# Fewer, larger last transfers, the last V product ahead of the MLP product, and set-up work moved off VectorE, in a decode kernel of attention and MLP

## The chip, the cores and the metric

One NeuronCore of a Trainium2 chip runs the whole program, once. The metric is the device time of one execution in microseconds (us). Before the change three runs gave 722.03 to 722.25 us, median 722.1 us.

## The reference, cut to what matters

Two rows of `x` (B = 2) pass through a decode step of multi-head attention (32 heads of 128, 4096 cached keys and values for each head) and through a dense MLP with a tanh-approximated GELU; a sigmoid gate mixes the two.

```python
q = (x @ wq) split into 32 heads                       # x [2,1,576], wq [576,4096]
p = softmax(einsum("bhqd,bhkd->bhqk", q, k_cache) * 128**-0.5)   # k_cache [2,32,4096,128]
a = einsum("bhqk,bhkd->bhqd", p, v_cache) flattened @ wo         # wo [4096,576]
b = gelu(x @ w1 + b1) @ w2 + b2                        # w1 [576,4608], w2 [4608,576]
g = sigmoid((x * gate_w).sum(-1))
out = g * a + (1 - g) * b
```

All of it is fp32. The K and V caches are 134 MB each, the weights together 40 MB.

## The kernel before, in words

**One ring of three slots.** SBUF holds one tile `ring` with three slots of 64 KB per partition. The weights wq and w1 fill its front first. After that every transfer of the list `seq` takes the next slot: K and V of unit 0, of unit 1, up to unit 15 (a unit is four heads of one batch row, 8.4 MB of K and as much of V), and last three slots named in `LAST`, which hold w2 and wo. All these transfers are issued from SyncE (SP) in that order. A transfer may be issued when the slot that it writes is free: `load_next` is called behind the work that reads a slot for the last time. The first `LAST` slot takes V of unit 14's place, the second K of unit 15's, the third V of unit 15's.

**A unit.** VectorE multiplies K with q in place (`mul`, L510), GpSimd halves a part of the product (L514), VectorE adds up the rest (`red`, L515 and L516) and takes the maximum (L520); TensorE turns it (`mt`, L525), ScalarE takes the exponentials into the tile `p` (`softmax`, L535), and TensorE multiplies them with V in 32 matmuls of 512 columns (`av`, L546; a matmul in fp32 shows as two passes, so 64). `keep` (L558) and `combine` (L564) fold the result into the tile `oall`. The product with V of unit k is made beside the K work of unit k + 1.

**The set-up.** SP issues wq and w1 in five transfers, ScalarE (ACT) issues the first part of b1, the two rows of x and gate_w. x is transposed on TensorE (`xps`, L270) once gate_w is there, then come the projections to q (`qps`, L303) and to the MLP's hidden row (`hps`, L303), with the GELU in `hg`. Constants such as `idsc`, the zeroed `p` and `rs` and `ones` are made on VectorE.

**The separate half row of w2.** The last of each partition's 36 rows of w2 is loaded only in its first half as part of the block; the other halves (128 half rows of 288) are loaded apart, into `XP` partitions with `XS` half rows in each (`wx`, from `XC` transfers over `XE` partitions). The hidden values that belong to them have to be laid out the same way, in `hx`: before, VectorE makes the two patterns `mod` and `div` and the masked product `hm`, and one matmul gathers it (L416).

**The tail.** After the 15th unit's `max_n` and `softmax` TensorE's program is written out by hand: `mlp_out(lo, hi)` multiplies hg with rows lo to hi of w2 (four passes a row), `mlp_x` does the separate half rows (two passes each), `norm_sum`, `norm_t` and `o_turn` normalise and turn the attention output between pieces of `mlp_out`, `wo_out(0, 23)` multiplies it with the first 23 rows of wo, and `last_out` does rows 23 to 31 into `res` and writes the output. All of `mlp_out`, `mlp_x` and `wo_out` are line L367 with the tile `acc`.

Of the kernel before, what the change touches and what calls it, by code (L numbers as in the profile page):

```python
# [8 lines left out]
F32 = mybir.dt.float32  # L9
AF = mybir.ActivationFunctionType  # L10
ALU = mybir.AluOpType
AX = mybir.AxisListType
P = 128
# [6 lines left out]
def kernel(  # L20
# [14 lines left out]
    nc = tc.nc  # L35
    B, H, SK, DH = k_cache.shape
# [21 lines left out]
    NF = F // P  # L58
# [4 lines left out]
    SCALE = float(DH) ** -0.5  # L63
# [1 line left out]

    LAST = (
        (("w2", 0, 14), ("w2", 14, 28)),
        (("w2", 28, 36), ("wx", 0, 1), ("wo", 0, 8), ("wo", 8, 16)),
        (("wo", 16, 23), ("wo", 23, 27), ("wo", 27, 30), ("wo", 30, 31), ("wo", 31, 32)),
    )  # L70
    FOLD = 23
    SLOT = R * DH
# [17 lines left out]
    ps_sm = ctx.enter_context(tc.tile_pool(name="ps_sm", bufs=3, space=bass.MemoryType.PSUM))  # L90
# [18 lines left out]
    def load_w(w, rows, c):  # L109
        if c < len(rows):  # L110
            n = rows[c] * w.shape[1]
            lo = sum(rows[:c]) * P
            src = w[lo:lo + rows[c] * P].rearrange("(p r) n -> p (r n)", r=rows[c])
        else:
            n = w.shape[1] // 2
            src = w[NX * P:].rearrange("q (e n) -> (q e) n", e=2)
        t = ring[:, used["w"]:used["w"] + n]
        used["w"] += n
        nc.sync.dma_start(t, src)
        return t  # L120
# [5 lines left out]
    def load_heads(src, i):  # L126

        t = slot(SLOT)
        h = i // B * E
        nc.sync.dma_start(t, src[i % B, h:h + E].rearrange("h (p r) d -> (h p) (r d)", p=PE_))  # L130
        return t.rearrange("p (r d) -> p r d", d=DH)

    srcs = {"w2": w2.rearrange("(p r) n -> p (r n)", r=NF), "wo": wo.rearrange("(p r) n -> p (r n)", r=32)}

    XE, XC = 4, 4
    XP = XE * XC
    XS = P // XP
    srcx2 = w2.rearrange("(e c s r) n -> c r e s n", e=XE, c=XC, s=XS)[:, NF - 1, :, :, DS:]
# [4 lines left out]
    def load_last(m):  # L143
        n = sum(length(*q) for q in LAST[m])

        used["e"], used["z"] = len(held) % SLOTS * SLOT + n, (len(held) % SLOTS + 1) * SLOT
        t = slot(n)
        o = 0
        for w, a, z in LAST[m]:
            if w == "wx":  # L150
                xt = t[:XP, o:o + XS * DS]
                rows[w] = xt.rearrange("p (s n) -> p s n", s=XS)
                o += XS * DS
                for c in range(XC):
                    nc.sync.dma_start(xt[c::XC].rearrange("e (s n) -> e s n", s=XS), srcx2[c])
                continue
            if (w, z) == ("w2", NF):
                nc.sync.dma_start(t[:, o:o + length(w, a, z)], srcs[w][:, a * D:z * D - DS])
                for r in range(a, z):
                    rows[w, r] = t[:, o + (r - a) * D:o + min((r - a + 1) * D, length(w, a, z))]  # L160
                o += length(w, a, z)
                continue

            ends = (a * D, a * D + DS, a * D + DS + DO, z * D) if (w, z) == ("wo", 32) else (a * D, z * D)
            for u, v in zip(ends, ends[1:]):
                nc.sync.dma_start(t[:, o:o + v - u], srcs[w][:, u:v])
                o += v - u
            for r in range(a, z):
                rows[w, r] = t[:, o - (z - r) * D:o - (z - r - 1) * D]

    def temp(n, parts=P):
        t = ring[:parts, used["t"]:used["t"] + n]
        used["t"] += n
        assert used["t"] <= SLOTS * SLOT
        return t

    def late(n, parts=P):
        t = ring[:parts, used["e"]:used["e"] + n]
        used["e"] += n
        assert not seq and used["e"] <= used["z"]  # L180
        return t

    def load():
        if not seq:
            return
        kind, i = seq.pop()
        if kind == "wq":
            wqt[i] = load_w(wq, ROWS[kind], i)
        elif kind == "w1":
            w1t[i] = load_w(w1, ROWS[kind], i)  # L190
        elif kind == "k":
            kt[i] = load_heads(k_cache, i)
        elif kind == "v":
            vt[i] = load_heads(v_cache, i)
        else:
            load_last(i)
        if kind in ("k", "v", "last"):
            held.append((kind, i))
# [7 lines left out]
    xg = temp(D, B + 1)  # L206
# [8 lines left out]
    def load_b1(b):  # L215
        nc.scalar.dma_start(b1r.rearrange("(g q) n -> g q n", g=NG)[:, b], b1.rearrange("(g n) -> g n", g=NG))


    load_b1(0)
    for b in range(B):  # L220
        nc.scalar.dma_start(xg[b:b + 1], x[b])
    nc.scalar.dma_start(xg[B:B + 1], gate_w[None, :])
    load()
    load()
# [2 lines left out]
    ident = cp.tile([P, P], F32, name="ident")  # L227
    make_identity(nc, ident)
    ones = cp.tile([P, 1], F32, name="ones")
    nc.vector.memset(ones, 1.0)  # L230
    idsc = cp.tile([P, P], F32, name="idsc")
    nc.vector.tensor_scalar_mul(idsc, ident, SCALE)


    NPB = 1
# [3 lines left out]
    pt = []  # L239
    for j in range(NPB):  # L240
        t = cp.tile([P, NT * EB + 32 - EB], F32, name=f"p{j}")
        nc.vector.memset(t, 0.0)
        pt.append(t)
    rs = cp.tile([P, NO], F32, name="rs")
    nc.vector.memset(rs, 0.0)


    sel = ident.rearrange("p (j c) -> p j c", j=4)[:, :, :EB].rearrange("p j (e r) -> p j e r", e=E)
# [114 lines left out]
    def acc_mm(lhsT, rhs, k, start=False, stop=False, lo=0):  # L363
        m = lhsT.shape[-1]
        for s in range(lo, lo + rhs.shape[-1] // DS):
            o = 64 * (k % 2) + 32 * s
            nc.tensor.matmul(  # L367
                acc[o:o + m], lhsT, rhs[:, (s - lo) * DS:(s - lo + 1) * DS], start=start, stop=stop, skip_group_check=True
            )
# [19 lines left out]
    for m, ps in enumerate(hps):  # L389
# [7 lines left out]
    hg = cp.tile([P, NF, B], F32, name="hg")  # L397
    t = temp(NF * B).rearrange("p (r b) -> p r b", b=B)
# [5 lines left out]
    nc.vector.tensor_mul(t, t, hb)  # L404
    nc.vector.tensor_mul(hg, t, g1.unsqueeze(1).to_broadcast([P, NF, B]))

    mod = temp(XS)
    nc.vector.tensor_reduce(mod, ident.rearrange("p (q s) -> p s q", s=XS), AX.X, ALU.add)
    div = temp(XP)
    nc.vector.tensor_reduce(div, ident.rearrange("p (q s) -> p q s", s=XS), AX.X, ALU.add)  # L410
    hm = temp(XS * B).rearrange("p (s b) -> p s b", b=B)
    nc.vector.tensor_mul(
        hm, hg[:, NF - 1:].to_broadcast([P, XS, B]), mod.unsqueeze(2).to_broadcast([P, XS, B])
    )
    hxps = ps_sm.tile([XP, XS * B], F32, tag="sm", name="hxps")
    nc.tensor.matmul(hxps, div, hm.rearrange("p s b -> p (s b)"), start=True, stop=True)  # L416
    hx = cp.tile([XP, XS, B], F32, name="hx")
    nc.vector.tensor_copy(hx.rearrange("p s b -> p (s b)"), hxps)
    load()

    def mlp_x():
        for s in range(XS):
            acc_mm(hx[:, s], rows["wx"][:, s], s, lo=1)

    def mlp_out(lo, hi):
        for r in range(lo, hi):
            acc_mm(hg[:, r], rows["w2", r], r)
# [103 lines left out]
    def softmax(i):  # L531
        p = pt[i % NPB][:, :NT * EB].rearrange("p (t c) -> p t c", c=EB)
        for e in range(E):
            w = slice(e * PE_, (e + 1) * PE_)
            nc.scalar.activation(  # L535
                p[w, :, e * RB:(e + 1) * RB], st[i][w].rearrange("p (t c) -> p t c", c=RB), AF.Exp,
                bias=bias[i][w, e:e + 1], scale=SCALE, accum_out=rs[w, i * E + e:i * E + e + 1],
            )


    def av(i):
        ps = ps_av.tile([P, 512], F32, tag="av", name=f"av{i}")
        p = pt[i % NPB]
        for t in range(NT):
            j = t % 4
            nc.tensor.matmul(  # L546
                ps[32 * j:32 * j + 32],
                p[:, EB * t:EB * t + 32],
                vt[i][:, RB * t:RB * (t + 1)].rearrange("p r d -> p (r d)"),
                start=(t < 4),  # L550
                stop=(t >= NT - 4),
            )
        avs[i] = ps


    def keep(i):
        t = ep.tile([P, RB, DH], F32, tag="avs", name=f"avs{i}")
        nc.vector.tensor_mul(  # L558
            t, avs[i].rearrange("p (r d) -> p r d", d=DH), selr.unsqueeze(2).to_broadcast([P, RB, DH])
        )  # L560
        avs[i] = t

    def combine(i):
        nc.tensor.matmul(  # L564
            oall, pick[:, NO - E - i * E:2 * NO - E - i * E], avs[i].rearrange("p r d -> p (r d)"),
            start=(i == 0), stop=(i == N - 1), skip_group_check=True,
        )
# [38 lines left out]
    k = N - 1  # L606
    max_n(k)
    softmax(k)
    mlp_out(0, 24)
    av(k)  # L610
    load_next(("v", k))
    assert not seq
    keep(k)
    combine(k)
    turn = late(P)
    nc.vector.tensor_copy(turn.rearrange("p (h k) -> p k h", k=KB), ident.rearrange("p (k h) -> p k h", k=KB))
    osum = late(DH, NO)
    norm_sum()
    mlp_out(24, 30)
    norm_t()  # L620
    mlp_out(30, 33)
    o_turn(turn)
    mlp_out(33, NF)
    mlp_x()
    wo_out(0, FOLD)
    last_out()
# [28 lines left out]
```

## Time and profile before

| what | value |
|---|---|
| runs | 722.25, 722.03, 722.1 us; median 722.1 |
| the profiled execution | 722.19 us, of which the span from the first to the last instruction is 720.0 us |
| TensorE, VectorE, ScalarE, GpSimd busy | 235.7, 518.3, 37.8, 143.2 us |
| granted TensorE clock, mean | 0.663 |
| read from HBM | 308.59 MB |

A row of the timeline has the start in us from the span's start, the time in us, the engine, the line, the operation, the tiles and the number of instructions merged into it; in square brackets stands how long the engine was idle ahead of it and what ended that. "SPq" is SyncE's sequencer, which issues transfers, "PEld" TensorE's weight load. A row of the chain of work has start, time and what. A row of the windows has the stretch, its length, busy us of each engine, then the granted clock, the mean share of the 16 DMA engines that is busy, and GB/s. A row of the DMA queues has packets, MB, and their share of the 16 engines' span.

### The profile page before, as it was taken

What the parts mean: (1) busy time and instruction counts of PE and PEld (TensorE: products, weight loads), DVE (VectorE), ACT (ScalarE), POOL (GpSimd) and SP (SyncE); (2) the same over time, 40 slices, a digit from 0 to 9 for tenths busy, and PEclk for the clock granted to TensorE, in tenths of its full rate; (3) what the DMA queues carried; (4) which work ended last, traced back from release to release, by engine and by line L of the source; (5) the groups of instructions that cost most, each with busy time, mean ns of one, the idle gap of its engine ahead of it and who ended that gap; (6) DMA issues with size and microseconds to landing.
All of it is one profiled execution on the core that took longest, in us unless ns stands there. A gap on an engine that the chain in (4) does not pass through costs nothing.

```text
span 720.0 us, 3946 instructions
## 1 busy us (share of the span) xinstructions
PE 235.7 (33%) x1681; PEld 72.8 (10%) x1681; DVE 518.3 (72%) x154; ACT 37.8 (5%) x141; POOL 143.2 (20%) x28
## 2 busy tenths in 40 slices
PE   0646013140516060604143140506070503223188
PEld 0322000010101010101010010101010101000023
DVE  0003969879696969696969879696969596978900
ACT  0010010100001010101010100101010101010000
POOL 1000040404050403022140404040503113040400
PEclk9967557575757575566657575757575665757599
DMA  9999999999999999999999999999999999999997
GB/s 409 412 443 434 433 437 419 451 420 448 426 448 420 437 437 419 442 430 441 434 433 441 430 431 433 437 430 431 441 430 444 427 444 426 433 430 438 415 426 303
DMA packets 7245, 308.84 MB, mean 429 GB/s; under 512 B 814, under 2 KB 1326, under 8 KB 1596
## 3 DMA queue, kind: packets, MB, share of 16 engines
q1 hardware_dynamic: 7204, 308.55, 99.2%
q8 instruction: 13, 0.21, 0.1%
q10 hardware_dynamic: 24, 0.05, 0.0%
q14 instruction: 4, 0.03, 0.0%
HBM read 308.59 MB, written 0.00 MB: 429 GB/s over the span
## 4 chain that ended last, share of the span: by engine, by line
DMA 45%; DVE 35%; PE 17%; ACT 1%; issue 1%; POOL 0%; ACTq 0%; DVEq 0%; SPq 0%; POOLq 0%
DMA ring<-in_A_k_cache_dram 34%; DVE ring L510 19%; DVE s L515 10%; PE av L546 10%; DMA ring<-in_B_w_dram 5%; DVE s L516 5%; DMA ring<-in_gate_w_dram 3%; DMA ring<-in_A_wo_dram 3%; PE hps L303 2%; PE qps L303 1%; ACT p L535 1%; PE oall L564 1%; DMA ring<-in_B_b_dram 1%; PE mt L525 1%; PE acc L367 1%
## 5 line engine op out<-in xcount | busy, mean ns | idle before, releaser
L510 DVE TENSOR_TENSOR ring<-ring,q 128x16384 f32<-128x16384 f32 x16 | 275.6, 17224 | 100.2 <-DMA ring<-in_A_k_cache_dram 100.2
L514 POOL TENSOR_TENSOR ring<-ring 128x3968 f32<-128x3968 f32 x16 | 137.0, 8564 | 486.9 <-DVE ring L510 419.1
L515 DVE TENSOR_REDUCE s<-ring 128x66 f32<-128x8448 f32 x16 | 143.2, 8953 | 1.3
L546 PE MATMUL av<-ring,p 128*32 128x512 f32 x1024 | 132.6, 676 | 11.4 <-ACT p L535 6.1
L525 PE MATMUL mt<-idsc,m 128*128 128x128 f32 x32 | 12.7, 500 | 359.4 <-DVE m L520 359.4
L516 DVE TENSOR_REDUCE s<-ring 128x62 f32<-128x3968 f32 x16 | 68.4, 4276 | 0.0
L535 ACT ACTIVATE p<-s,bs 32x128 f32<-32x128 f32 x64 | 25.5, 398 | 481.8 <-DVE bs L529 480.6
L546 PEld LDWEIGHTS av<-ring,p 128*32 128x32 f32 x1024 | 35.6, 124 | 118.1 <-issue 101.3
L525 PEld LDWEIGHTS mt<-idsc,m 128*128 128x128 f32 x32 | 8.0, 312 | 375.0 <-DVE m L520 316.7
L351 PE MATMUL qb<-qm,spread 64*128 64x512 f32 x8 | 8.3, 1138 | 71.5 <-POOL qm L347 71.5
L564 PE MATMUL oall<-avs,pick 128*64 128x512 f32 x32 | 30.6, 1059 | 0.8 <-DVE avs L558 0.8
L558 DVE TENSOR_TENSOR avs<-av,selr 128x512 f32<-128x512 f32 x16 | 10.9, 681 | 16.3 <-PE av L546 16.3
L390 DVE TENSOR_TENSOR ring<-hps,ring 128x384 f32<-128x384 f32 x3 | 1.7, 559 | 17.9 <-PE hps L303 17.7
L261 DVE COPY ring<-ring 3x64 f32<-3x64 f32 x2 | 0.3, 182 | 19.2 <-DMA ring<-in_gate_w_dram 19.2
L347 POOL TENSOR_TENSOR qm<-qall,mine 64x512 f32<-64x512 f32 x4 | 4.1, 1032 | 46.3 <-ACT qall L330 46.3
L322 DVE COPY ring<-ident 128x8 f32<-128x8 f32 x8 | 0.7, 171 | 16.8 <-DMA ring<-in_B_b_dram 16.8
L303 PE MATMUL hps<-ring 128*32 128x384 f32 x120 | 11.9, 564 | 0.0
L535 ACT ACTIVATION_READ_ACCUMULATOR p<-s,bs 32x1 f32 x64 | 11.8, 184 | 0.0
L367 PE MATMUL acc<-ring,hg 128*2 128x288 f32 x142 | 10.6, 423 | 1.2 <-DMA ring<-in_B_w_dram 1.2
L303 PE MATMUL qps<-ring 128*32 128x512 f32 x80 | 10.3, 677 | 0.0
L351 PEld LDWEIGHTS qb<-qm,spread 64*128 64x128 f32 x8 | 2.0, 308 | 74.6 <-POOL qm L347 74.6
L481 DVE COPY ring<-res 2x144 f32<-2x144 f32 x1 | 0.3, 297 | 12.4 <-PE res L461 12.4
(92 smaller groups left out, 78.5 us busy)
## 6 DMA issues: line engine op xcount, KB each, us to landing
ring<-in_B_w_dram SPq DMA_DIRECT2D x2, 4608.0 KB
ring<-in_B_w_dram SPq DMA_DIRECT2D x2, 4032.0 KB
ring<-in_A_wo_dram SPq DMA_DIRECT2D x2, 2304.0 KB
ring<-in_B_w_dram SPq DMA_DIRECT2D x1, 2160.0 KB, 13.4
ring<-in_A_wo_dram SPq DMA_DIRECT2D x1, 2016.0 KB
ring<-in_B_w_dram SPq DMA_DIRECT2D x1, 1152.0 KB
ring<-in_A_wo_dram SPq DMA_DIRECT2D x1, 1152.0 KB, 17.6
ring<-in_A_wq_dram SPq DMA_DIRECT2D x1, 1024.0 KB, 24.0
```

Source lines behind the costliest of these rows:

```text
L303: nc.tensor.matmul(ps[32 * j:32 * j + 32, :width], lhs, ts[c][:, o:o + width], start=(k == 0), stop=last, skip_group_check=True,)
L351: nc.tensor.matmul(ps, spread, t.rearrange("p u d -> p (u d)"), start=True, stop=True)
L367: nc.tensor.matmul(acc[o:o + m], lhsT, rhs[:, (s - lo) * DS:(s - lo + 1) * DS], start=start, stop=stop, skip_group_check=True)
L510: nc.vector.tensor_mul(kt[i], kt[i], qs[i].unsqueeze(1).to_broadcast([P, R, DH]))
L514: nc.gpsimd.tensor_add(t[:, :, :DH2], t[:, :, :DH2], t[:, :, DH2:])
L515: nc.vector.tensor_reduce(st[i][:, HALVED:], kt[i][:, HALVED:], AX.X, ALU.add)
L516: nc.vector.tensor_reduce(st[i][:, :HALVED], t[:, :, :DH2], AX.X, ALU.add)
L525: nc.tensor.matmul(mt[i], mx[i].to_broadcast([P, P]), idsc, start=True, stop=True)
L535: nc.scalar.activation(p[w, :, e * RB:(e + 1) * RB], st[i][w].rearrange("p (t c) -> p t c", c=RB), AF.Exp, bias=bias[i][w, e:e + 1], scale ...
L546: nc.tensor.matmul(ps[32 * j:32 * j + 32], p[:, EB * t:EB * t + 32], vt[i][:, RB * t:RB * (t + 1)].rearrange("p r d -> p (r d)"), start=(t ...
L558: nc.vector.tensor_mul(t, avs[i].rearrange("p (r d) -> p r d", d=DH), selr.unsqueeze(2).to_broadcast([P, RB, DH]))
L564: nc.tensor.matmul(oall, pick[:, NO - E - i * E:2 * NO - E - i * E], avs[i].rearrange("p r d -> p (r d)"), start=(i == 0), stop=(i == N - ...
```

## The change

Five edits:

1. wo's rows 0 to 7, 8 to 15 and 16 to 22 came in three transfers, the first two in the second `LAST` slot, the third in the third slot. Now rows 0 to 11 come in one, in the second slot, and rows 12 to 22 in one, in the third.
2. The separate half row of w2 (`wx`) lies in 8 partitions with 16 half rows each (before 16 with 8) and comes in two transfers instead of four; `mlp_x` has 16 matmuls instead of 8.
3. The two rows of x come in one transfer instead of two.
4. `ones`, `p` and `rs` are set on GpSimd, `idsc` on ScalarE. `mod`, `div` and `hm` are gone: 16 small matmuls gather the hidden values with slices of the identity, ScalarE copies them to `hx`, and K of unit 1 is asked for ahead of them.
5. In the tail `av` of the last unit stands first on TensorE, ahead of every `mlp_out`, and `mlp_out` is cut at other rows.

```diff
     LAST = (
         (("w2", 0, 14), ("w2", 14, 28)),
-        (("w2", 28, 36), ("wx", 0, 1), ("wo", 0, 8), ("wo", 8, 16)),
-        (("wo", 16, 23), ("wo", 23, 27), ("wo", 27, 30), ("wo", 30, 31), ("wo", 31, 32)),
+        (("w2", 28, 36), ("wx", 0, 1), ("wo", 0, 12)),
+        (("wo", 12, 23), ("wo", 23, 27), ("wo", 27, 30), ("wo", 30, 31), ("wo", 31, 32)),
     )
...
-    XE, XC = 4, 4
+    XE, XC = 4, 2
...
-    for b in range(B):
-        nc.scalar.dma_start(xg[b:b + 1], x[b])
+    nc.scalar.dma_start(xg[:B], x.rearrange("b s d -> (b s) d"))
...
-    nc.vector.memset(ones, 1.0)
+    nc.gpsimd.memset(ones, 1.0)
...
-    nc.vector.tensor_scalar_mul(idsc, ident, SCALE)
+    nc.scalar.mul(idsc, ident, SCALE)
...
-        nc.vector.memset(t, 0.0)
+        nc.gpsimd.memset(t, 0.0)
...
-    nc.vector.memset(rs, 0.0)
+    nc.gpsimd.memset(rs, 0.0)
...
-    mod = temp(XS)
-    nc.vector.tensor_reduce(mod, ident.rearrange("p (q s) -> p s q", s=XS), AX.X, ALU.add)
-    div = temp(XP)
-    nc.vector.tensor_reduce(div, ident.rearrange("p (q s) -> p q s", s=XS), AX.X, ALU.add)
-    hm = temp(XS * B).rearrange("p (s b) -> p s b", b=B)
-    nc.vector.tensor_mul(
-        hm, hg[:, NF - 1:].to_broadcast([P, XS, B]), mod.unsqueeze(2).to_broadcast([P, XS, B])
-    )
-    hxps = ps_sm.tile([XP, XS * B], F32, tag="sm", name="hxps")
-    nc.tensor.matmul(hxps, div, hm.rearrange("p s b -> p (s b)"), start=True, stop=True)
+    load()
+
+    hxps = ps_sm.tile([XP, XS, B], F32, tag="sm", name="hxps")
+    for s in range(XS):
+        nc.tensor.matmul(
+            hxps[:, s], ident.rearrange("p (q s) -> p s q", s=XS)[:, s], hg[:, NF - 1], start=True, stop=True
+        )
     hx = cp.tile([XP, XS, B], F32, name="hx")
-    nc.vector.tensor_copy(hx.rearrange("p s b -> p (s b)"), hxps)
-    load()
+    nc.scalar.copy(hx, hxps)
...
-    mlp_out(0, 24)
     av(k)
     load_next(("v", k))
     assert not seq
     keep(k)
+    mlp_out(0, 5)
     combine(k)
...
     norm_sum()
-    mlp_out(24, 30)
+    mlp_out(5, 12)
     norm_t()
-    mlp_out(30, 33)
+    mlp_out(12, 19)
     o_turn(turn)
-    mlp_out(33, NF)
+    mlp_out(19, NF)
     mlp_x()
```

On TensorE in the tail, from `combine` of unit 14 (the first row) to `wo_out` (the last), the program before reads as follows (`acc<-ring,hg` is `mlp_out`, `hx` is `mlp_x`, `oP` is `wo_out`, x48 are 48 matmuls):

```order
L564 MATMUL oall<-avs_1159,pick 64x512
L367 MATMUL acc<-ring,hg 2x288 x48
L546 MATMUL av_1216<-ring,p_114 32x512 x32
L564 MATMUL oall<-avs_1256,pick 64x512
L572 MATMUL psum<-ones,rs 64x1
L367 MATMUL acc<-ring,hg 2x288 x12
L581 MATMUL oT_t<-ident,ring 128x64
L367 MATMUL acc<-ring,hg 2x288 x6
L439 MATMUL op_t<-ring 128x64
L367 MATMUL acc<-ring,hg 2x288 x5
L367 MATMUL acc<-ring,hx 2x288 x8
L367 MATMUL acc<-ring,oP 2x288 x46
```

At the same place in the changed program:

```order
L559 MATMUL oall<-avs_1167,pick 64x512
L541 MATMUL av_1176<-ring,p_113 32x512 x32
L366 MATMUL acc<-ring,hg 2x288 x10
L559 MATMUL oall<-avs_1216,pick 64x512
L567 MATMUL psum<-ones,rs 64x1
L366 MATMUL acc<-ring,hg 2x288 x14
L576 MATMUL oT_t<-ident,ring 128x64
L366 MATMUL acc<-ring,hg 2x288 x14
L434 MATMUL op_t<-ring 128x64
L366 MATMUL acc<-ring,hg 2x288 x33
L366 MATMUL acc<-ring,hx 2x288 x16
L366 MATMUL acc<-ring,oP 2x288 x46
```

The 32 matmuls of the last V product have moved ahead of all of `mlp_out`; 71 matmuls of `mlp_out` stand behind it where 23 stood, and `mlp_x` has grown from 8 to 16.

On SyncE, the transfers behind the first `LAST` slot, before (rows of each partition's shape; the last five are wo's rows 23 to 31):

```order
L158 DMA ring<-in_B_w_dram 128x4320
L155 DMA ring<-in_B_w_dram 4x8x288 x4
L166 DMA ring<-in_A_wo_dram 128x4608 x2
L166 DMA ring<-in_A_wo_dram 128x4032
L166 DMA ring<-in_A_wo_dram 128x2304
L166 DMA ring<-in_A_wo_dram 128x1728
L166 DMA ring<-in_A_wo_dram 128x576
L166 DMA ring<-in_A_wo_dram 128x288
L166 DMA ring<-in_A_wo_dram 128x144 x2
```

And in the changed program:

```order
L158 DMA ring<-in_B_w_dram 128x4320
L155 DMA ring<-in_B_w_dram 4x16x288 x2
L166 DMA ring<-in_A_wo_dram 128x6912
L166 DMA ring<-in_A_wo_dram 128x6336
L166 DMA ring<-in_A_wo_dram 128x2304
L166 DMA ring<-in_A_wo_dram 128x1728
L166 DMA ring<-in_A_wo_dram 128x576
L166 DMA ring<-in_A_wo_dram 128x288
L166 DMA ring<-in_A_wo_dram 128x144 x2
```

Two transfers of `wx` and one of wo are gone with the bytes and their order unchanged; the first transfer that needs V of unit 15's slot is now that of rows 12 to 22 instead of 16 to 22.

On ScalarE at the program's start, before, from its first transfer to the first copy of `qps`:

```order
L216 DMA ring<-in_B_b_dram 4x1152
L221 DMA ring<-in_A_x_dram 1x576 x2
L222 DMA ring<-in_gate_w_dram 1x576
L282 ACT_TABLE_LOAD
L282 ACTIVATE gb<-zps 128x2
L313 COPY ring<-qps_152 128x512
```

And in the changed program:

```order
L216 DMA ring<-in_B_b_dram 4x1152
L220 DMA ring<-in_A_x_dram 2x576
L221 DMA ring<-in_gate_w_dram 1x576
L231 ACT_TABLE_LOAD
L231 ACTIVATE idsc<-ident 128x128
L281 ACTIVATE gb<-zps 128x2
L312 COPY ring<-qps_151 128x512
```

One transfer fewer stands ahead of gate_w, and `idsc` has come in behind it.

## The prediction

> **What bounds the kernel now.** I read the page's head and DMA queues first, then windows over start, middle and end, then the chain of work.
>
> ```profile
> span 720.0 us, 3946 instructions
> ...
> q1 hardware_dynamic: 7204, 308.55, 99.2%
> ```
>
> SyncE's queue kept the 16 DMA engines busy for 99.2% of the span: 714.2 of 720.0 us. All that is not streaming adds up to 5.8 us. Three windows show where that lies, and two more look into the tail (column before the last: DMA share).
>
> ```profile
> 0.00:2.50 2.50, 0.00 (x0) 0.00 (x0) 0.23 (x2) 0.00 (x0) 1.90 (x8) 1.00 1.22 419
> 2.50:715.50 713.00, 233.92 (x1641) 71.87 (x1644) 517.51 (x151) 37.28 (x139) 141.30 (x21) 0.66 1.00 432
> 715.50:720.00 4.50, 1.75 (x44) 0.96 (x44) 0.60 (x2) 0.55 (x2) 0.00 (x0) 0.96 0.08 26
> 690.00:700.00 10.00, 9.19 (x104) 2.88 (x96) 0.74 (x2) 0.00 (x0) 0.00 (x0) 1.00 1.01 428
> 700.00:715.40 15.40, 14.76 (x201) 5.93 (x201) 2.08 (x9) 0.40 (x1) 0.00 (x0) 1.00 0.96 403
> ```
>
> From 2.5 to 715.5 us the engines are full, at 432 GB/s. The only slack is the 4.5 us behind the last bytes. The chain of work ends in those:
>
> ```profile
> 654.35 35.32 DMA ring<-in_B_w_dram
> ...
> 692.32 3.50 PE av L546 x32
> ...
> 696.19 19.25 DMA ring<-in_A_wo_dram
> ...
> 715.48 1.52 PE res L461 x36
> 717.00 0.28 DVE ring L481
> 717.29 0.32 DVEq L650
> ```
>
> So the time is the bytes at 432 GB/s, plus what TensorE, VectorE and the output transfer need after wo's last rows. The change leaves all 308.6 MB and their order. It can gain or lose only in that tail, or by letting the engines run dry.
>
> **The start: x in one transfer, set-up off VectorE.** These rows are from SyncE's waits (us in total, times, longest), the chain and the timeline:
>
> ```profile
> SPq L119 <- DMA ring<-in_B_b_dram: 8.4, 1, 8.4
> ...
> SPq L119 <- DMA ring<-in_A_x_dram: 4.6, 1, 4.6
> ```
> ```profile
> 3.52 19.48 DMA ring<-in_gate_w_dram
> ...
> 69.67 0.23 DVE hg L405
> ...
> 70.53 0.25 PE hxps L416 x2
> ...
> 102.23 0.78 PE mt L525 x2
> ```
> ```profile
> 3.68 0.27 DVE L259 MEMSET ring<- 3x256 f32 x1
> ...
> 35.67 0.34 SPq L130 DMA_DIRECT2D ring<-in_A_k_cache_dram  x1
> ...
> 62.63 0.33 SPq L130 DMA_DIRECT2D ring<-in_A_v_cache_dram  x1
> ```
>
> ScalarE's transfers land one behind another: SyncE waited 8.4 us for b1 and 4.6 us more for the first row of x; gate_w came at 23.0. One transfer fewer brings gate_w 2.5 to 4.9 us earlier (the lower end: half a step, as the last step was shorter). TensorE's projections, K of unit 0 (35.67) and V of unit 0 (62.63) then go out earlier. Nothing is gained: the weights wq and w1 are 39168 floats per partition, 20.05 MB, 46.4 us at 432 GB/s from 2.5, so until 48.9; K of unit 0 keeps the engines until 68.3. Both requests come 13 and 6 us before the queue would run dry. That is also the cover: the start may lose 6 us before it costs anything.
>
> The set-up that leaves VectorE was done by 3.95, in front of a wait until 23; on GpSimd and ScalarE it has the same 19 us. The 16 small matmuls for `hx` follow `hg` at 70 us, when TensorE has nothing until the first `mt` at 102; at the 0.25 us of the one that they replace they take 4. The VectorE steps that go lay beside the transfer of V of unit 0. Sum for the start: 0, ends minus 0.2 and plus 0.2.
>
> **The larger transfers.** One x, two `wx` and one wo transfer fewer. While the queue is full a transfer's setup is hidden by its neighbours, so this is 0; the cost if each had a gap would be seen as a share under 1.00, and the windows 690 to 700 have 1.01. In 700 to 715.4 the share is 0.96: 0.6 us is missing there, mostly because the engines do not finish together. That is the most that transfers asked for earlier could give: minus 0.6 to 0. I take minus 0.1.
>
> **The last V product first.** What the third slot waits for is `av` of unit 15. Before, it stood behind 48 matmuls of `mlp_out`; its first 32 passes, those that read what the third slot's first transfer overwrites, ended at 692.32 + 3.50 = 695.8. Now it starts when the last exponential is done, and wo's rows 12 to 22 are asked for some 7 us earlier. But at 696.19 there were (715.43 - 696.19) us x 432 GB/s = 8.3 MB to come, and the third slot is 16 rows, 4.7 MB: 3.6 MB of the second slot were still queued. The queue was 8 us deep, so asking earlier gains nothing.
>
> What the move can do is make TensorE late. Its rows before:
>
> ```profile
> 684.86 0.18 ACT L535 ACTIVATION_READ_ACCUMULATOR p<-s,bs 32x1 f32 x1
> ...
> 689.72 2.61 PE L367 MATMUL acc<-ring,hg 128*2 128x288 f32 x40 [1.22 <-DMA ring<-in_B_w_dram]
> ...
> 692.14 7.05 PE L546 MATMUL av<-ring,p 128*32 128x512 f32 x64
> ...
> 700.00 1.07 PE L564 MATMUL oall<-avs,pick 128*64 128x512 f32 x2 [0.81 <-DVE avs L558]
> ...
> 701.07 1.64 PE L367 MATMUL acc<-ring,hg 128*2 128x288 f32 x24
> ...
> 702.64 0.27 PE L581 MATMUL oT_t<-ident,ring 64*128 64x64 f32 x1
> ...
> 702.84 1.14 PE L367 MATMUL acc<-ring,hg 128*2 128x288 f32 x12
> ...
> 703.91 0.44 PE L439 MATMUL op_t<-ring 128*128 128x64 f32 x2
> ...
> 704.27 1.13 PE L367 MATMUL acc<-ring,hg 128*2 128x288 f32 x10
> ...
> 705.33 2.10 PE L367 MATMUL acc<-ring,hx 16*2 16x288 f32 x16
> ...
> 707.37 5.99 PE L367 MATMUL acc<-ring,oP 128*2 128x288 f32 x92
> ...
> 713.40 1.17 PE L461 MATMUL res<-ring,oP 128*2 128x144 f32 x32
> ...
> 714.38 0.43 PE L471 MATMUL res<-ring,fold 128*2 128x144 f32 x8
> ...
> 715.48 1.47 PE L461 MATMUL res<-ring,oP 128*2 128x144 f32 x36 [0.67 <-DMA ring<-in_A_wo_dram]
> ...
> 716.76 0.49 PE L485 MATMUL res<-ring,oP 128*2 128x72 f32 x8
> ```
>
> A pass of `mlp_out` takes (692.14 - 689.72) / 40 = 0.0605 us. The new order, start to start: `av` from 685.1 (684.86 + 0.18 and a step of 0.1); `mlp_out` 20 passes 1.2; `oall` and `psum` 1.07 (their wait for VectorE's `avs` is now under the 20 passes); 28 passes 1.7; `oT_t` 0.2; 28 passes 1.7, plus 0.35 of switching (702.84 to 703.91 is 1.07 for 12 passes, 0.73 of work); `op_t` 0.36; 68 passes 4.1, plus 0.45 of switching (704.27 to 705.33 is 1.06 for 10 passes); `mlp_x` 32 passes at twice 2.04, less one switch, 4.0; `wo_out` 92 passes 5.6. With 0.2 for small gaps that is 20.9 us behind `av`. How long is `av`? It is 7.05 above, behind running matmuls. Behind a pause it is longer; the 15 earlier ones took from 7.54 to 9.73; the longest, the shortest and the middle one:
>
> ```profile
> 297.81 9.73 PE L546 MATMUL av<-ring,p 128*32 128x512 f32 x64 [0.71 <-issue]
> ...
> 336.35 7.54 PE L546 MATMUL av<-ring,p 128*32 128x512 f32 x64 [0.66 <-issue]
> ...
> 529.45 8.26 PE L546 MATMUL av<-ring,p 128*32 128x512 f32 x64 [0.61 <-ACT p L535]
> ```
>
> Now the last `av` also starts behind a pause of about 0.6 us, so I take the middle one, 8.26, and keep both ends. Of these times 0.2 overlap with what follows. `res` then starts at 685.1 + 8.1 + 20.9 = 714.1 (ends 713.4 and 715.6), against 713.40 before. It may start as late as 715.48 - 0.98 - 0.25 = 714.25 without cost: the 32 passes up to `fold` take 0.98, the 8 of `fold` at the same rate 0.25, and what comes behind them waits for wo's rows 27 to 29 at 715.48. So the middle case just fits, the shortest leaves 0.85 us, the longest is 1.35 us late. `mlp_x`, doubled, is 2.0 us of this: without that edit even the longest `av` would fit. The value I take is plus 0.2.
>
> On that spread the Trainium skill, "TensorE: Matmul & The Clock Gate", Part 1, says that the array runs at half rate until a free-running window of about 3.4 us has been busy. By that page the penalty would be at most half of some 3.4 us plus what the window missed, an `av` of about 8.8; the sum above would then come out 0.4 us late. The rows agree in kind, but 9.73 is longer than that.
>
> **The sum.** Start 0, transfers minus 0.1, tail plus 0.2: 722.2 us. The profiled execution was 722.19 us, its span 720.0 and 2.2 around it, 0.1 over the median of 722.1; the profile stands for the runs, and I predict 722.2.
>
> **The rivals.**
> *TensorE becomes the end of the tail.* The place is `res`: each us that it starts behind 714.25 is a us on the end, since all of wo has landed by then. For it: the doubled `mlp_x`, 71 instead of 23 matmuls of `mlp_out` behind `av`, and the 9.73 row. Against it: the middle `av` fits. Price: 1.35 us for the longest `av` alone, 723.5; with half a us more of switching around the new `mlp_out` pieces 724.0. To be slower by over 0.2% (1.44 us, to 723.54 and above; about what a measurement of this kernel can tell from no change) `res` has to start after 715.7. 14%.
> *The earlier start counts.* If VectorE's first unit, not the queue, set the rhythm, gate_w 2.5 to 4.9 us earlier would show at the end: 717.2 to 719.6. Against it: the share of 1.00 over 713 us. 3%.
> *Fewer transfers save their fixed cost.* The output transfer, 4.5 KB, is issued about 717.7 and the span ends at 720.0: at most 2.3 us for an almost empty transfer. Were the four removed ones each in line, that is 9.2 us, 712.9. Against it again the share of 1.00. 2%. The Trainium skill, "DMA: Bandwidth & Descriptors", Rules for kernel authors, does say to coalesce many small transfers into one; by that rule this rival would be the likely one.
> *The forecast*, end set by the bytes, TensorE on time or up to 1.4 us late, or the tail's 0.6 us of missing share recovered: 721.5 to 723.5. 81%.
>
> **How the numbers follow.** Likeliest 722.2. Faster is the second and third rival, 5%. Within 0.2% (720.7 to 723.5) is the forecast, 81%. Slower is the first rival, 14%. The range goes from 721.4 (0.6 recovered, 0.2 for the start) to 723.8 (into the first rival, most of it): it leaves the two faster rivals and the end of the slow one outside.
>
> **What would show it.** Right: SyncE's queue again at about 99.2% of the span; gate_w at 18 to 20.5; `av` of unit 15 starting at 685 and wo's third transfer issued before 690 with its landing still near 710; `res` starting near 714 and its second group still waiting for wo near 715.5. The slow rival shows as no idle time on TensorE from 685 to the last `res`. Wrong altogether: a queue share that differs by more than 0.1%, or a share well under 1.00 in the windows 690 to 700 or 2.5 to 715.5.

## The result, and the profile after

| what | before | after |
|---|---|---|
| median (lowest to highest) | 722.1 us (722.03 to 722.25) | 725.12 us (724.81 to 725.73), 6 runs |
| the profiled execution, its span | 722.19, 720.0 us | 724.92, 723.1 us |
| granted TensorE clock, mean | 0.663 | 0.658 |

The change made the kernel slower by 3.0 us: ratio 1.0043, 95% interval 1.003 to 1.0056. The forecast was 722.2 us, with a range that ended at 723.8.

The page's head and SyncE's queue after, and then three windows (busy us of each engine, clock, DMA share, GB/s):

```profile
span 723.1 us, 4027 instructions
...
q1 hardware_dynamic: 7052, 308.55, 98.9%
```
```profile
715.50:723.10 7.60, 4.81 (x120) 2.72 (x112) 0.60 (x2) 0.95 (x3) 0.00 (x0) 1.00 0.15 50
690.00:700.00 10.00, 9.94 (x111) 3.59 (x103) 2.55 (x9) 0.00 (x0) 0.00 (x0) 1.00 1.01 378
700.00:715.40 15.40, 15.40 (x160) 5.13 (x163) 0.22 (x1) 0.00 (x0) 0.00 (x0) 0.78 0.98 414
```

The stretch behind 715.5 was 4.5 us and is now 7.6. Two other things changed. From 700 to 715.4 TensorE has no idle time at all, yet its clock is 0.78 where it was 1.00. And from 690 to 700 the engines are as full as before (1.01) but move 378 GB/s instead of 428. Smaller windows put that where the `wx` transfers come and wo's first behind them; the first pair is the changed kernel, the second the kernel before:

```profile
692.00:694.00 2.00, 2.00 (x32) 0.65 (x23) 0.69 (x1) 0.00 (x0) 0.00 (x0) 1.00 1.22 336
694.00:696.00 2.00, 2.00 (x20) 0.78 (x20) 0.02 (x1) 0.00 (x0) 0.00 (x0) 1.00 0.82 269
```
```profile
692.00:694.00 2.00, 2.00 (x28) 0.68 (x24) 0.00 (x0) 0.00 (x0) 0.00 (x0) 1.00 1.02 415
694.00:696.00 2.00, 2.00 (x24) 0.52 (x16) 0.00 (x0) 0.00 (x0) 0.00 (x0) 1.00 1.01 425
```

The timeline of TensorE, and the last piece of the chain of work, which was wo's transfer and `res` before:

```profile
685.40 7.52 PE L541 MATMUL av<-ring,p 128*32 128x512 f32 x64 [0.66 <-issue]
692.73 1.64 PE L366 MATMUL acc<-ring,hg 128*2 128x288 f32 x20
694.30 1.07 PE L559 MATMUL oall<-avs,pick 128*64 128x512 f32 x2
...
695.36 2.11 PE L366 MATMUL acc<-ring,hg 128*2 128x288 f32 x28
...
700.11 4.53 PE L366 MATMUL acc<-ring,hg 128*2 128x288 f32 x66
704.57 5.66 PE L366 MATMUL acc<-ring,hx 8*2 8x288 f32 x32
710.15 7.47 PE L366 MATMUL acc<-ring,oP 128*2 128x288 f32 x90
717.22 0.41 PE L456 MATMUL res<-ring,oP 128*2 128x144 f32 x4
```
```profile
700.18 17.33 PE acc L366 x187
```

`res` starts at 717.22 (713.40 before), and nothing on TensorE waits for wo any more: that is the place which the slow rival named. The clock, in windows laid on the steps at which it changes:

```profile
703.43:706.84 3.41, 3.41 (x36) 1.15 (x28) 0.00 (x0) 0.00 (x0) 0.00 (x0) 1.00 0.98 414
706.84:710.25 3.41, 3.41 (x20) 0.78 (x18) 0.00 (x0) 0.00 (x0) 0.00 (x0) 0.50 0.98 421
710.25:713.67 3.42, 3.42 (x32) 1.04 (x30) 0.00 (x0) 0.00 (x0) 0.00 (x0) 0.50 0.95 398
713.67:717.08 3.41, 3.41 (x64) 1.32 (x54) 0.00 (x0) 0.00 (x0) 0.00 (x0) 1.00 0.77 293
```

For 6.83 us TensorE is busy the whole time at half its clock. At full clock that work would take 3.41 us, so 3.4 us are lost. The first of these four windows holds 2.27 us of `mlp_x`, whose matmuls use 8 rows of the array, and the clock falls at its end; `mlp_x` fills the second up to 710.15, and the clock stays down in the third; `wo_out`, on all 128 rows, fills the third, and the clock is back in the fourth.

### The profile page after: what moved, and what is told of

Same layout as the page of the kernel before. It is cut to its first block, busy times and chain, and to the rows that moved or that the text cites. A ratio compares the mean times of both kernels' runs of the same rounds, so it can differ in the third digit from the quotient of the medians.

```text
span 723.1 us, 4027 instructions
## 1 busy us (share of the span) xinstructions
PE 244.9 (34%) x1727; PEld 75.8 (10%) x1727; DVE 516.9 (71%) x146; ACT 38.3 (5%) x143; POOL 143.8 (20%) x31
## 3 DMA queue, kind: packets, MB, share of 16 engines
q1 hardware_dynamic: 7052, 308.55, 98.9%
## 4 chain that ended last, share of the span: by engine, by line
DMA 43%; DVE 35%; PE 20%; issue 1%; ACT 1%; POOL 0%; DVEq 0%; ACTq 0%; SPq 0%; POOLq 0%
DMA ring<-in_A_k_cache_dram 39%; DVE ring L505 19%; DVE s L510 10%; PE av L541 9%; DVE s L511 5%; PE acc L366 3%; DMA ring<-in_gate_w_dram 2%; PE hps L302 2%; PE oall L559 1%; PE qps L302 1%; DMA ring<-in_B_b_dram 1%; PE mt L520 1%; ACT p L530 1%; PE qps L327 1%; DVE m L515 0%
## 5 line engine op out<-in xcount | busy, mean ns | idle before, releaser
L541 PE MATMUL av<-ring,p 128*32 128x512 f32 x1024 | 136.6, 693 | 12.1 <-ACT p L530 6.2
```

The costliest lines, as they stand in the source:

```text
L541: nc.tensor.matmul(ps[32 * j:32 * j + 32], p[:, EB * t:EB * t + 32], vt[i][:, RB * t:RB * (t + 1)].rearrange("p r d -> p (r d)"), start=(t ...
```

## The experiments

The theories in the expectations are these. A, the clock: a long stretch of matmuls that fill few of the array's 128 rows, as `mlp_x` now is, halves the clock and makes TensorE late. B, plain length: TensorE is late because `mlp_x` has twice as many passes. C, the transfers: two larger `wx` transfers, or the larger wo transfers, make wo land later. All kernels start from the changed one unless something else is said; "ratio" is against the kernel before in the same session.

### 16 partitions again, the rest of the change kept

```diff
-    XE, XC = 4, 2
+    XE, XC = 4, 4
```

> The changed kernel with the separate half row of w2 back in 16 partitions and four transfers (mlp_x has 8 matmuls of 16 rows again), everything else as changed. Theory A, the clock: a whole window of matmuls on only 8 rows of the array lets the clock fall to half, and TensorE is 3 us late: without them the clock stays at 1.00 from 688 us to the end, mlp_x takes 2.0 us, and the time is 722.1 (721.8 to 722.4). Theory B, plain length: the tail on TensorE is too long at any clock, by the V product first and the extra matmuls: 2 us of mlp_x go, 723.1. Theory C, the transfers: the two transfers into 8 partitions crowd the DMA engines and wo's last rows land later: 722.1 too, with wo's last rows landing about 1 us earlier than in the changed kernel.

721.71 us, ratio 0.9993 (0.9984 to 1.0002). The timeline, and windows over the `wx` transfers and behind them:

```profile
705.43 2.10 PE L366 MATMUL acc<-ring,hx 16*2 16x288 f32 x16
707.46 6.04 PE L366 MATMUL acc<-ring,oP 128*2 128x288 f32 x92
...
715.22 1.53 PE L456 MATMUL res<-ring,oP 128*2 128x144 f32 x36 [0.49 <-DMA ring<-in_A_wo_dram]
```
```profile
692.00:694.00 2.00, 2.00 (x28) 0.67 (x24) 0.05 (x1) 0.00 (x0) 0.00 (x0) 1.00 1.16 483
694.00:696.00 2.00, 2.00 (x22) 0.70 (x15) 0.83 (x2) 0.00 (x0) 0.00 (x0) 1.00 1.04 438
704.00:712.00 8.00, 8.00 (x114) 2.90 (x106) 0.00 (x0) 0.00 (x0) 0.00 (x0) 1.00 0.97 410
```

The whole loss is in edit 2: the clock is 1.00, `res` waits for wo's last rows again, and the bytes set the end. Everything else in the change together is worth at most the 0.5 us by which this is under the kernel before in the same session (722.17 us).

### The same 16 matmuls, padded with zeros to 128 rows

```diff
-                rows[w] = xt.rearrange("p (s n) -> p s n", s=XS)
+                rows[w] = t[:, o:o + XS * DS].rearrange("p (s n) -> p s n", s=XS)
...
-    hx = cp.tile([XP, XS, B], F32, name="hx")
-    nc.scalar.copy(hx, hxps)
+    hx = cp.tile([P, XS, B], F32, name="hx")
+    nc.gpsimd.memset(hx, 0.0)
+    nc.scalar.copy(hx[:XP], hxps)
```

> The changed kernel with hx padded with zeros to 128 rows, so that mlp_x has the same 16 matmuls in the same place over 128 rows of the array. A, if what keeps the clock up is how many rows of the array a matmul uses: clock 1.00, mlp_x 4.0 us, 723.0 (722.4 to 723.4). A, if zeros do not count as activity: the clock falls as in the changed kernel, 725. B: 725. C: 725.

722.49 us, ratio 1.0004 (0.9995 to 1.0014). Same number of passes and same transfers as the changed kernel; 120 of 128 rows of `hx` are zero.

```profile
692.00:694.00 2.00, 2.00 (x24) 0.66 (x20) 0.00 (x0) 0.00 (x0) 0.00 (x0) 1.00 1.15 324
694.00:696.00 2.00, 2.00 (x26) 0.73 (x18) 0.97 (x2) 0.00 (x0) 0.00 (x0) 1.00 1.03 358
...
704.00:712.00 8.00, 8.00 (x113) 3.46 (x109) 0.00 (x0) 0.00 (x0) 0.00 (x0) 1.00 0.96 409
```
```profile
716.53 0.85 PEld L457 LDWEIGHTS res<-ring,oP 128*2 128x2 f32 x32 [0.35 <-DMA ring<-in_A_wo_dram]
```

The clock stays at 1.00 and 2.6 of the 3.0 us are back: theory A. B is not the cause of these 2.6, since the passes are as many. What is left is 0.8 us over the version on 16 partitions. TensorE waits for wo again, but until 716.53 instead of 715.22, and the rate behind the `wx` transfers is 324 and 358 GB/s instead of 483 and 438 at full engines. So C sets the end here, but B stands close behind it: the wait was only 0.35 us, so TensorE itself was ready at 716.18, already 0.96 us after 715.22. This run does not divide the 0.8 us between them.

### How many rows, and for how long

Two kernels pad to 32 and to 64 rows (the code above with 32 or 64 for 128).

> The changed kernel with hx padded with zeros to 32 rows, mlp_x 16 matmuls in the same place. If the clock follows the rows that a matmul uses, 32 are nearer to the 16 that let it fall (16 matmuls over 16 rows gave 724.68) than to the 128 that held it: clock 0.50 for at least 3.4 us behind mlp_x, 724.5. If 32 rows are enough: 722.5, as with 128.

> The same with 64 rows. If the clock follows the rows in use, this lies between: held at 1.00 gives 722.5, fallen gives 724.5; no side is favoured.

A third goes back to 16 partitions and runs `mlp_x` twice, the second time with zeros `hz`, so that the 16-row stretch is as long as the 8-row one.

```diff
+        for s in range(XS):
+            acc_mm(hz[:, s], rows["wx"][:, s], s, lo=1)
```

> The changed kernel with the half row in 16 partitions, and mlp_x done a second time with weights of zero: 16 matmuls again, but each over 16 rows of the array. A, if a stretch of 4 us on few rows is enough: the clock falls as in the changed kernel, 724.5. A, if 16 rows are enough to keep it up: clock 1.00, mlp_x 4.0 us, TensorE about 1 us late, 722.8. B: 722.8 at a clock of 1.00 or not. C: 721.7, as with 16 partitions alone.

Padded to 32 rows 723.44 us (722.44 to 725.59), ratio 1.0018 (1.0007 to 1.0028); to 64 rows 722.79 us, ratio 1.0008 (0.9998 to 1.0018); 16 rows twice 724.68 us, ratio 1.0039 (1.0025 to 1.0052). The clock in the last part of `mlp_x` and behind it, for 32 rows and then for 64, and the timeline of 16 rows twice:

```profile
708.00:710.00 2.00, 2.00 (x14) 0.45 (x14) 0.00 (x0) 0.00 (x0) 0.00 (x0) 0.55 0.95 408
710.00:712.00 2.00, 2.00 (x20) 0.59 (x16) 0.00 (x0) 0.00 (x0) 0.00 (x0) 0.50 0.87 369
```
```profile
708.00:710.00 2.00, 2.00 (x24) 0.68 (x24) 0.00 (x0) 0.00 (x0) 0.00 (x0) 1.00 1.00 429
710.00:712.00 2.00, 2.00 (x40) 0.85 (x32) 0.00 (x0) 0.00 (x0) 0.00 (x0) 1.00 0.89 377
```
```profile
706.97 2.84 PE L366 MATMUL acc<-ring,hz 16*2 16x288 f32 x16
709.74 8.35 PE L366 MATMUL acc<-ring,oP 128*2 128x288 f32 x90
```

In these traces four us on 8 or 16 rows let the clock fall; on 64 or 128 they did not; two us on 16 rows (before, and the first experiment) did not. Both the share of the array and the length of the stretch count. Zero weights, as in `hz`, do not explain it: with 128 rows most weights were zeros too.

The place of the stretch seems to count as well. In the traces' clock records the clock changes at multiples of one 3.41 us step, and that grid lies differently in each run. A step that held 2.27 us on 8 rows (the changed kernel), 3.17 on 16 (twice) or 3.13 on 32 was followed by a fall; one with 1.99 us on 16 rows (the first experiment) or 3.41 on 64 was not. So the version on 16 partitions, whose `mlp_x` is 2.0 us long, may not have been far from a fall; no run shows where the bound lies. At 32 rows the eight runs fall into two groups: four from 722.44 to 722.72, as with 128 rows, and four from 724.16 to 725.59. The profiled one, 725.42, is of the second group and shows the fall; that the first group is without it was not seen in a trace, nor whether the grid decides between them.

### The old order on TensorE with the new half row

`mlp_out(0, 24)` stands ahead of `av` again, and the pieces are cut at 24, 30 and 33 as before.

> The changed kernel with TensorE's old order in the tail: 48 matmuls of mlp_out ahead of the last V product and 23 behind it; transfers and mlp_x (16 matmuls on 8 rows) as changed. A, the clock: mlp_x fills a window here too, the clock falls to half, TensorE is late by as much as in the changed kernel: 724.5 to 725.5. B, plain length: the V product first is part of the excess, so this gains: 723.5 with the clock as it may be. C, the transfers: 725.

724.81 us (723.93 to 726.03), ratio 1.0041 (1.0028 to 1.0054). Timeline and windows:

```profile
705.32 4.04 PE L366 MATMUL acc<-ring,hx 8*2 8x288 f32 x32
709.29 7.42 PE L366 MATMUL acc<-ring,oP 128*2 128x288 f32 x90
```
```profile
708.00:710.00 2.00, 2.00 (x20) 0.60 (x20) 0.00 (x0) 0.00 (x0) 0.00 (x0) 0.83 0.88 370
710.00:712.00 2.00, 2.00 (x20) 0.60 (x16) 0.00 (x0) 0.00 (x0) 0.00 (x0) 0.50 0.99 422
```

The order on TensorE neither caused the loss nor could it mend it. Here the clock fell just behind `mlp_x`, which kept its 4.04 us, and only `wo_out` paid, for one step of 3.41 us. The six times fall into two groups, 723.93 to 724.08 and 725.55 to 726.03; the profiled run, 724.01, is of the first. That those of the second lost two steps, as the changed kernel did, would fit, but none of them was profiled.

### Breaking up the few-row stretch

```diff
-    mlp_out(19, NF)
-    mlp_x()
+    mlp_out(19, NF - XS)
+    for s in range(XS):
+        mlp_out(NF - XS + s, NF - XS + s + 1)
+        acc_mm(hx[:, s], rows["wx"][:, s], s, lo=1)
```

> The changed kernel with the 16 matmuls of mlp_x put one by one between the last 16 rows of mlp_out; same work, same transfers. A, the clock: no window is filled by matmuls on 8 rows, the clock stays at 1.00, TensorE reaches wo about 3 us earlier: 722.6 (722.1 to 723.0), any rest being the transfers. B, plain length: the same number of passes, 725 or, with more switching, 726. C, the transfers alone: 725.

732.36 us, ratio 1.0143 (1.0128 to 1.0158): a miss, but the clock stayed at 1.00 as A wants. The timeline shows another price:

```profile
701.28 0.64 PE L366 MATMUL acc<-ring,hx 8*2 8x288 f32 x2
701.86 0.65 PE L366 MATMUL acc<-ring,hg 128*2 128x288 f32 x4
702.44 0.64 PE L366 MATMUL acc<-ring,hx 8*2 8x288 f32 x2
```

Each piece takes 0.58 us from start to start, two passes of `mlp_x` or four of `mlp_out`. Back to back, 32 passes of `mlp_x` took 3.97 us at full clock (705.32 to 709.29 in the kernel with the old order), 0.124 each, and a pass of `mlp_out` takes 0.0605, so both pieces have 0.24 to 0.25 us of work. That leaves some 0.33 us for each change between 8-row and 128-row matmuls, 32 times: 10.6 us, where the kernel took 9.9 more than the padded one. The Trainium skill, "TensorEngine Tiling (Array Packing)", Key Properties, says that a change of tiling mode drains TensorE. The price fits that, but the trace shows only the price; that such a change is one of tiling mode was not shown.

### Fewer transfers, or fewer partitions

The last part, 0.8 us. First `mlp_x` was left out of the changed kernel, and then also the 8 partitions were put four apart (the half rows of w2 are missing from the result in both).

> The changed kernel without mlp_x (the products with the separate half row are left out; its two transfers into 8 partitions stay). TensorE is then early, and wo's last rows alone set the end. A and B alone: 721.7, as with 16 partitions. C: the transfers into 8 partitions cost 0.8 us of their own: 722.5, and wo's transfer behind them takes longer per packet.

> As the one before (mlp_x left out, two transfers of 64 half rows into 8 partitions), but the 8 partitions lie 4 apart (0, 4, ..., 28) instead of side by side. C, if the crowding comes from neighbouring partitions: it is gone, 721.7. C, if it comes from two larger transfers or from few partitions anywhere: 722.5 still.

723.43 us, ratio 1.0019 (1.0009 to 1.0029), and 722.88 us, ratio 1.0009 (1.0 to 1.0019). The first and then the second timeline:

```profile
711.59 4.53 PE L366 MATMUL acc<-ring,oP 128*2 128x288 f32 x42 [3.42 <-DMA ring<-in_A_wo_dram]
```
```profile
711.13 4.12 PE L366 MATMUL acc<-ring,oP 128*2 128x288 f32 x42 [3.60 <-DMA ring<-in_A_wo_dram]
```

Spreading the partitions brings wo's rows 12 to 22 0.46 us earlier, in one trace of each. The times themselves do not serve: without `mlp_x` TensorE idles for 3.4 us, and the clock fell for that (0.50 from 712 to 714 in the first).

Then the number of transfers was parted from the number of partitions: `XE, XC = 8, 2` for 16 partitions in two transfers, and `XE, XC = 2, 4` with the padding to 128 rows for 8 partitions in four. Both also change how many partitions one transfer writes: 8 and 2, where the change and the first experiment have 4.

> The changed kernel with the separate half row on 16 partitions, but in two transfers instead of four (8 matmuls with hx). It parts the number of transfers from the number of partitions, for the 0.8 us by which the zero-padded kernel stayed above the version on 16 partitions. If the partitions crowd the engines: 721.7 us, the engines' rate in 692 to 696 us near 440 to 480 GB/s, the last group of res waiting for wo at about 715.2. If it is that two transfers stand where four did: 722.5 us, the rate near 320 to 360 GB/s there, and res waiting at about 716.5. TensorE's clock stays at 1.00 in both, since the stretch on 16 rows is 2 us.

> The zero-padded kernel (8 partitions, 16 matmuls, hx padded with zeros to 128 rows), with the half row in four transfers instead of two. If 8 partitions crowd the engines whatever the number of transfers: 722.5 us, 320 to 360 GB/s in 692 to 696 us, res waiting for wo at about 716.5. If the two transfers were the cause: 721.8 us, 440 to 480 GB/s and 715.3. The clock stays at 1.00 in both.

722.9 us, ratio 1.0009 (1.0 to 1.0018), and 722.47 us, ratio 1.0004 (0.9995 to 1.0013): neither is at 721.7. Windows, and the wait for wo's last rows, of the first and then of the second:

```profile
692.00:694.00 2.00, 2.00 (x30) 0.79 (x24) 0.69 (x1) 0.00 (x0) 0.00 (x0) 1.00 1.16 354
694.00:696.00 2.00, 2.00 (x20) 0.68 (x16) 0.00 (x0) 0.00 (x0) 0.00 (x0) 1.00 1.04 385
```
```profile
717.15 1.49 PE L456 MATMUL res<-ring,oP 128*2 128x144 f32 x36 [0.49 <-DMA ring<-in_A_wo_dram]
```
```profile
692.00:694.00 2.00, 2.00 (x25) 0.63 (x21) 0.00 (x0) 0.00 (x0) 0.00 (x0) 1.00 1.07 440
694.00:696.00 2.00, 2.00 (x22) 0.75 (x15) 0.89 (x2) 0.00 (x0) 0.00 (x0) 1.00 0.95 404
```
```profile
716.33 1.54 PE L457 MATMUL res<-ring,oP 128*2 128x144 f32 x36 [0.31 <-DMA ring<-in_A_wo_dram]
```

The lowered rate goes with two transfers (354 and 385 GB/s on 16 partitions), not with 8 partitions (440 and 404 with four transfers). The packet records of the traces say the same: the 128 half rows take 51 ns each in every kernel with four transfers, and on average 72 in the changed kernel and 62 on 16 partitions in two (56 with 8 partitions four apart); the large packets that start beside them take 59 and 47 ns a KB, where four transfers have 38 to 39. With `mlp_x` as short as before, the two transfers then cost 1.2 us by themselves (722.9 against 721.7; the kernel before took 722.2 and 722.28 in the two sessions). Why they slow what runs beside them stays open.

The kernel with 8 partitions in four transfers is late all the same, and for another reason: its engines end unevenly. Half of the packets of wo's rows 27 to 29 have landed at 712.69 and the last at 715.98; with 16 partitions in four transfers it was 712.85 and 714.80. The half rows move two at a time there (16 of them start within 0.38 us) and four at a time on 16 partitions (0.19 us). Our estimate from these: 128 packets of 51 ns are 3.3 us for each of two engines, 1.6 us for each of four, so two engines finish some 1.6 us behind where they would have. That would make it the 2 partitions of each transfer, not the 8 in all; no run separates the two. Here too TensorE was ready only 0.31 us before its wait ended, so the 0.8 us are not the transfers' alone.

### Two that went elsewhere

The kernel before with `XE, XC = 4, 2`, and the changed kernel with `XE, XC = 4, 8` (32 partitions, eight transfers).

> The kernel before with only the separate half row changed to 8 partitions and two transfers (16 matmuls in mlp_x), the old order on TensorE. A, the clock: it falls behind mlp_x here too, wo_out takes 7 us or more, 724.5 (723.5 to 725). B, plain length: 2.0 us more on TensorE less the 0.7 it waited before: 723.4 with the clock at 1.00. C, the transfers alone: 723.

> The changed kernel with the half row in 32 partitions, eight transfers, mlp_x 4 matmuls over 32 rows: the opposite direction. TensorE has 1.0 us less than with 16 partitions, the wo landing is as there: it waits for wo, 721.7 as with 16 partitions (721.4 to 722.1). If eight small transfers cost the queue something: 722.5.

The first, 743.26 us, tells nothing of the cost: on 8 partitions `wx` takes 4608 floats of the slot, and with w2's block and wo's rows 0 to 15 that makes 4320 + 4608 + 9216 = 18144 of a slot's 16384, so the second `LAST` slot ran into V of unit 15, which wo overwrote before `av` had read it. `av` stood in wait of wo for 14.87 us. That is why edit 1 belongs to edit 2: four rows of wo had to leave that slot. The clock fell behind this kernel's `mlp_x` too, to 0.50 from 725.06 to 731.89, after a step with 2.54 us on 8 rows.

The second, 727.27 us (ratio 1.007, 1.0056 to 1.0084), is a miss of another kind. SyncE's waits, windows, and TensorE's timeline:

```profile
SPq L155 <- DMA ring<-in_B_w_dram: 7.4, 2, 4.5
```
```profile
692.00:694.00 2.00, 2.00 (x24) 0.57 (x20) 0.00 (x0) 0.00 (x0) 0.00 (x0) 1.00 0.47 176
694.00:696.00 2.00, 2.00 (x26) 0.68 (x19) 0.69 (x1) 0.00 (x0) 0.00 (x0) 1.00 0.00 0
```
```profile
715.19 4.87 PE L366 MATMUL acc<-ring,oP 128*2 128x288 f32 x42 [5.11 <-DMA ring<-in_A_wo_dram]
```

In the program a transfer that SyncE issues waits for the eighth one before it: in the trace the seventh `wx` transfer goes out at 689.73 and the eighth at 694.81, each behind the w2 transfer eight places ahead. Eight small ones in a row so use up the look-ahead: SyncE stood 7.4 us on earlier w2 transfers, wo was asked for 10 us later, and the engines had nothing from 694 to 696.

### The better version, once more

> The changed kernel with 16 partitions once more, in five rounds, to see whether the rest of the change is a gain over the kernel before: 721.7, that is 0.4 us or 0.06% under it, by wo's last rows landing earlier; or no difference, 722.1, if the first batch's chip made it.

721.7 us (721.43 to 721.91, 11 runs) against 722.28 for the kernel before: ratio 0.9991 (0.9982 to 1.0). The change with the half row left as it was is 3.4 us under the change, and some 0.6 us under the kernel before, with an interval that just reaches 1.

## Why the prediction was wrong

- **Bytes set the end: right for the kernel before and for the version on 16 partitions, not after.** The queue's share fell to 98.9%, by 0.3 points, where "what would show it" called more than 0.1 wrong altogether, and TensorE ended the tail.
- **The start, 0: right.** The chain and SyncE's timeline after have gate_w landing at 20.3 and K of unit 0 going out at 33.06 instead of 35.67; nothing came of either. The set-up on GpSimd and ScalarE cost nothing that shows.

```profile
3.27 17.07 DMA ring<-in_gate_w_dram
```
```profile
33.06 0.34 SPq L130 DMA_DIRECT2D ring<-in_A_k_cache_dram  x1
```

- **The last V first: right.** `av` started at 685.40; wo's rows 12 to 22 were asked for at 689.49, and wo came hardly earlier for it, even on 16 partitions (the wait of `res` ended at 715.22 instead of 715.48). That `av` took 7.52 us, just under the shortest of the earlier ones, was luck: the same code took 8.60 in the first experiment and 8.98 in the padded kernel. This spread was the wrong place to look for the loss. The rule of the Trainium skill that the prediction cited for it ("TensorE: Matmul & The Clock Gate", Part 1), half rate until a window has been busy, was near the cause, but on the wrong matmuls.
- **The step that failed: "`mlp_x` 32 passes at twice 2.04 … 4.0; `wo_out` 92 passes 5.6".** It carried rows taken at full clock over to the doubled stretch, and put nothing for the clock, which that stretch halved for 6.83 us. Start to start they took 5.6 and 7.1 us, 3.1 us more. The first two pieces of `mlp_out` (1.57 us up to `oall`, and 2.11) came out 0.8 longer than the sum had, which the shorter `av` gave back. With `res` at 717.22 instead of 714.1 the end moved as the slow rival had priced it: one us for each us behind 714.25, so 3.0.
- **The slow rival had the right place and the wrong price.** "TensorE becomes the end of the tail" held at 14%, with 1.35 us for a long `av` and half a us of switching. The doubled `mlp_x` was named for it, but only by its 2.0 us of plain length; that length alone is not it, as 128 rows show.
- **"The larger transfers", minus 0.1: wrong sign for `wx`.** It rested on "while the queue is full a transfer's setup is hidden by its neighbours", and on a share of 1.01 as the sign of no cost. The share stayed at 1.01, with 50 GB/s less moved: packets took longer. On 16 partitions two transfers instead of four measured plus 1.2 us; in the change itself the cost is hidden behind the clock, since the last packet of wo's rows 27 to 29 landed at 716.20, 1.40 us later than in the first experiment, and `res` started at 717.22. The rule of the Trainium skill, "DMA: Bandwidth & Descriptors", Rules for kernel authors, to coalesce many small transfers into one, which the fewer-transfers rival was weighed with, did not hold for these four.

The Trainium skill, "TensorE: Matmul & The Clock Gate", Part 1, gives a free-running window of 3413 ns and a fall to half rate after an idle one. The steps of 3.41 us agree; here the clock fell on a TensorE which was never idle, which that rule does not cover, and the measurement decides.

## What to carry to other kernels

When the layout of a matmul is changed so that it uses fewer rows and more passes, cost it twice: the passes, and the clock behind them. Here 2.3 us or more of a 3.41 us step on 8 to 32 of 128 rows halved the clock for what followed, and zero rows up to 64 or 128 were a cheap cure, where alternating with full matmuls was a dear one (732.36 us). And read a full DMA queue by its GB/s beside its share: here the share was 1.01 both times while the rate fell from 428 to 378 GB/s.

## What was not expected of the hardware

- The clock followed how much of the array worked: TensorE busy without a gap on 8 or 16 rows, and once on 32, for 4 us fell to 0.50 for one or two windows of 3.41 us; on 64 or 128 rows it stayed at 1.00, though the added rows were zeros.
- A change between 8-row and 128-row matmuls cost some 0.33 us.
- Two transfers in place of four, of the same bytes into the same 16 partitions (eight of them in each transfer instead of four), lowered what all engines moved for 4 us from 460 to 370 GB/s, at a share of 1.10 both times.
